# Expert routing by digits: where the running digit sum is formed and compared, and which engine makes some of the low weight parts

## The chip, the cores and the metric

The program runs on one core of a Trainium2 chip. The time is device microseconds of one execution. Five engines work at once, each through its own instructions in order: TensorE (PE in the profile, with PEld for its weight loads), VectorE (DVE), ScalarE (ACT), GpSimd (POOL) and SyncE (SP). TensorE writes its results to PSUM, which VectorE and ScalarE read.

## The reference

A bucketed attention makes 3072 tokens of 512 features, and a mixture of 8 experts works on them. Each expert takes at most 384 tokens: pairs of token and expert are visited from the highest logit down, and a token goes to the first expert that still has room.

```
x = attention(q, k, v, proj)                 # 3072 x 512, softmax within equal hash buckets
logits = x @ w_gate                          # 3072 x 8
for idx in argsort(-logits.flatten()):       # highest first
    tok, e = idx // 8, idx % 8
    if assigned[tok] >= 0 or counts[e] >= 384: continue
    assigned[tok] = e; counts[e] += 1
for e in range(8):
    h = maximum(x[assigned == e] @ w1[e], 0) # 384 x 1024
    out[assigned == e] = h @ w2[e]           # 384 x 512
```

## The kernel before

The first 403 us of the profiled execution are the attention and the logits. The diff adds only six small constants to that part. The rest is the mixture.

**Experts on TensorE.** `run` writes TensorE's program by hand: 68 slots per expert. In slots 0 to 31 `layer1` issues three matmuls of 128x384 each (four slots make one of eight pieces f of the hidden layer), in slots 32 to 67 `layer2` issues two of 128x512. Every product is made of half-precision high and low parts: for weights, `wsplit` lets ScalarE make the high part wh (L731) and scale the raw weights wf in place (L732), a quarter of a matrix at a time; the low part wl = wf - wh is made in halves of 512 columns by GpSimd (L743) or by VectorE (L747). The halves stand in the list `pend`: `hand` gives some of them to GpSimd behind a tiny copy ("tick") that waits for the latest comparison, and `fill` gives one to VectorE. The hidden piece f gets its high part hh from ScalarE (L783) and, four slots later (`lag`), its low part hl from VectorE (L784). The inputs xl (L757) are made likewise.

**Routing, one expert ahead.** While expert k's matmuls run, the generator `phase(k+1)` finds which tokens the next expert takes. It searches a threshold key in six digits (layers l = 0 to 5). Each digit is one loop round VectorE and TensorE: a comparison of the running value d with a table (`compare`, L497), a counting on TensorE (`count` for l = 0, `count4`, L515, for l = 1 to 5), three small subtractions (L517, L518), a test and a maximum (L593, L594) that give `hit`, and a matmul that sums `hit` over partitions (L597). From that sum n VectorE makes the new running value and compares again:

```
T.matmul(n,s.us[l][...],hit[...],start=True,stop=True)
V.scalar_tensor_tensor(d2,d,n,E[:,l+1],op0=ALU.subtract,op1=ALU.add)   # L603
s.compare(CMP[l+1],l+1,d2)
```

After the sixth counting (l = 5) come the last test (`satl`, L610), a matmul pair (L613, L614), a run of small VectorE steps to `cum` (L616 to L637), a matmul pair (L640, L641), the list of members (L649 to L662) and its collecting (L651), and the state for the next expert (L694, L667 to L673, then `best`).

**What sets the order.** The tables E1, EV, EO and ES say in which slot each of a phase's 14 to 18 pieces is issued; H1, H2 and HS how many halves GpSimd is handed after each; W1 and W2 in which slots ScalarE splits the quarters of the two matrices; XS and XD where the inputs are transposed. Each engine executes its share strictly in that order.

Of the kernel before, what the change touches and what calls it, by code (L numbers as in the profile page):

```python
# [378 lines left out]
SH=[25,20,15,10,5,0]  # L379
LOW=[1,1,1,1,1,0]  # L380
NT=[128,32,32,32,32,32]
E1=[-12,-4,-3,2,6,8,10,13,16,19,22,25,28,31,34,37,42,49]
H1=[0,0,0,0,0,2,0,2,0,2,0,3,0,3,0,0,0,0]
H2=[0,0,0,3,0,3,0,3,0,4,0,0,0,0]
EV=[0,0,-5,-8,-12]
ES=[-17,-14,-11,-8,-2,1,5,8,12,15,19,22,28,36]
EO=[0,3,6,9,13,16,20,23,27,30,34,37,43,51]
WL=[4,46]
W1=[[],[57,66,70,74],[53,65,69,73],[50,57,62,67],[46,52,58,63],[44,52,58,63]]
HS=[0,0,0,2,0,3,0,3,0,3,0,0,0,0]  # L390
# [8 lines left out]
class Moe:  # L399
    def __init__(s, tc, nc, ctx, N):  # L400
        s.tc,s.nc,s.N=tc,nc,N
        s.NC=NC=N//128; s.CAP=N//8
        s.cp=ctx.enter_context(tc.tile_pool(name="mcp",bufs=1)); s.zp=ctx.enter_context(tc.tile_pool(name="mzp",bufs=2))
        s.IDX={}; s.XG={}; s.W={}; s.WIX={}; s.late=[]; s.pend=[]; s.lag=[]; s.gate=None

    def consts(s):

# [135 lines left out]
    def phase(s,ph):  # L543
# [5 lines left out]
        def ps(): return s.ps0() if first and s.ps0 else s.ps()  # L549
# [3 lines left out]
        if not last:  # L553
# [13 lines left out]
            for l,w in enumerate(WID):  # L567
                tot+=w; u=2.0**-tot; cmp=CMP[l]
                yield
                pc=ps()  # L570
                if l==0 or first:
                    for c0,c1_ in blocks if first else ((0,NC),):
                        if l: s.compare(cmp,l,d,c0,c1_)
                        s.count(pc,P,cmp,l,c0,c1_)
                    if first:
                        if l==0: wp=s.wps(); s.warm(KW[7],wp)
                        s.warm(KW[0],wp)
                    for a,b in ((l+1,l+2),) if first else ((1,6),):
                        if a<6:
                            for q in range(a,b): s.digit(P,q,slice(0,NC))  # L580
                            if first: V.tensor_tensor(E[:,a:b],D[:,a:b],s.sc[:,a:b],op=ALU.mult)
                            else:
                                for q in range(a,b): nc.scalar.activation(E[:,q],D[:,q],AF.Copy,scale=2.0**-sum(WID[:q+1]))
                                if ph>3: s.fill()
                else:
                    nt=s.count4(pc,P,cmp)

                if l==5: break
                sat=t([128,8],BF,"sat"); hit=t([128,1],BF,"hit") if l==0 or first else s.hits[l%2]; J=NT[l]
                if l==0 or first:  # L590
                    V.tensor_scalar(sat[0:J],pc[0:J,0:8],0.0,0.0,op0=ALU.is_ge,op1=ALU.max,accum_out=hit[0:J])
                else:
                    V.tensor_tensor(sat[0:32],pc[96:128,24:32],nt,op=ALU.is_ge)  # L593
                    V.reduce_max(hit[0:32],sat[0:32],axis=AX.X)  # L594
                if not first: yield
                pn=ps(); n=pn[:,0:1]
                T.matmul(n,s.us[l][0:J if first else 128],hit[0:J if first else 128],start=True,stop=True)  # L597
                if first: s.warm(KW[1],wp)
                elif l==0 and ph>1:
                    s.fill()  # L600
                    if ph<4: s.fill()
                d2=t([128,NC],BF,"d2",bufs=6); s.gate=d2[0:1,0:1]
                V.scalar_tensor_tensor(d2,d,n,E[:,l+1],op0=ALU.subtract,op1=ALU.add)  # L603
                if not first:
                    s.compare(CMP[l+1],l+1,d2); s.gate=CMP[l+1][0:1,NC//2-1,0,0:1]
                d=d2

            sat=s.satl; s.gate=sat[0:1,0:1]; nn=t([128,1],F32,"nn"); nf=t([128,1],F32,"nf")
# [197 lines left out]
    def start(s):  # L806

        s.ps0=None; V=s.nc.vector
        s.wload(0,0,4,(0,1))
        next(s.ph0)  # L810
        s.gather(0)
        s.wload(0,0,4,(2,3))
        s.wsplit(0,0,0,V)
        next(s.ph0)
        s.ch=[s.phase(p) for p in range(8)]
        s.wsplit(0,0,1,V)
        s.wload(0,1,2)
        s.xsplit0()
        s.wsplit(0,0,2,by=14)
        s.wsplit(0,0,3,by=22)  # L820

    def run(s):
        V=s.nc.vector; ch=s.ch; at={}; NS=68
# [3 lines left out]
            if p<7: next(ch[p+1])  # L827
        def step(p,n):
            next(ch[p],None); s.hand(n)
        for p in range(1,8):  # L830
            b=NS*(p-1)
            c=[EV[p]+e for e in EO] if 1<p<5 else ES
            ev=[b+e for e in (E1 if p==1 else c)]
            hs=H1 if p==1 else H2 if p<4 else HS
            dec=ev[-3] if p<7 else b+24
            if p==7: ev=[b+28,b+40]; hs=[0,0]
# [4 lines left out]
                add(b+W1[min(p,5)][q],s.wsplit,p,0,q,None,b+NS+BY[0]+BY[1]*q if p<6 else 0)  # L841
                add(b+XS[q]+(XD[p] if p<4 else 0),s.xsplit,p,q)
        for k in range(8):
            for q in range(4): add(NS*k+W2[q],s.wsplit,k,1,q,None,NS*k+BY[2] if k<6 else 0)
            for q in range(3): add(NS*k+44+12*q+SC,s.scatter)
        for n in range(-NS,NS*8):
            s.now=n
            for f,a in at.get(n,()): f(*a)
            while s.lag and s.lag[0][0]<=n: s.lag.pop(0)[1]()
            while s.pend and s.pend[0][0]<=n: s.nc.gpsimd.tensor_tensor(*s.pend.pop(0)[1],op=ALU.subtract)  # L850
            if n<0: continue
            k,h=divmod(n,NS)
            if h<32: s.layer1(k,h//4,h%4)
            else: s.layer2(k,(h-32)//12,(h-32)%12)
# [53 lines left out]
```

## Time and profile before

| | |
|---|---|
| median of three runs | 749.07 us (747.76 to 753.79) |
| the profiled execution | 750.32 us, of which the trace spans 748.5 |
| TensorE matmul busy | 679.1 us, 91% of the span |
| VectorE, ScalarE, GpSimd busy | 541.0, 463.6, 511.7 us |
| mean granted TensorE clock | 0.969 |
| experts (from 433 us to the end of the span) | 315 us |

The engines work in parallel, so the busy times add up to more than the span. A matmul of 128x384 lasts 0.33 us from start to end, but the next one starts 0.16 us after it.

### The profile page before, as it was taken

To read this page: it belongs to the slowest core of one execution; us is meant where nothing else is said; L and a number is where in the kernel's file an instruction comes from. 1 tells how busy PE (TensorE), PEld (TensorE's weight loads), DVE (VectorE), ACT (ScalarE), POOL (GpSimd) and SP (SyncE) were. 2 spreads that over 40 slices of the span, in tenths; PEclk is the share of its full clock that TensorE was granted. 3 is DMA by queue.
4 is the path that set the end of the run, shared out by engine and by line. 5 is a ranking of instruction groups with operands and counts; after the bars stand their busy time and mean duration, and the time that the engine had idled before them with its cause. 6 is when DMAs were issued, how large, how long until landed. Compare 5 with 4: busy or idle time off the path is not lost. (4 is left out here: it accounts for less than half of the span.)

```text
span 748.5 us, 19027 instructions
## 1 busy us (share of the span) xinstructions
PE 679.1 (91%) x7789; PEld 437.9 (59%) x7789; DVE 541.0 (72%) x1162; ACT 463.6 (62%) x852; POOL 511.7 (68%) x452
## 2 busy tenths in 40 slices
PE   8898999999999999899997589999798999999995
PEld 2566666767667676677775454545445455555552
DVE  5879978887887899978875658586668878744120
ACT  7677676777767677566662171837456575666560
POOL 8686959798888878877663436575728392857671
PEclk9999999999999999999998589999999999999998
DMA  7638655427445264430000342525170717172611
GB/s 190 179 95 223 158 155 124 126 76 175 127 119 133 75 173 129 88 78 23 23 24 23 107 161 90 207 76 220 42 268 30 265 46 267 43 250 72 253 46 42
DMA packets 39951, 93.57 MB, mean 125 GB/s; under 512 B 4548, under 2 KB 30520, under 8 KB 37816
## 3 DMA queue, kind: packets, MB, share of 16 engines
q1 hardware_dynamic: 33048, 46.21, 23.7%
q0 software_dynamic: 6816, 46.15, 17.5%
q8 instruction: 61, 1.00, 0.6%
q14 instruction: 26, 0.21, 0.1%
HBM read 59.53 MB, written 12.58 MB: 96 GB/s over the span
## 5 line engine op out<-in xcount | busy, mean ns | idle before, releaser
L256 POOL TENSOR_TENSOR lo<-pt 128x768 f16<-128x768 f32 x143 | 234.5, 1652 | 57.0 <-ACT pt L253 48.6
L253 ACT ACTIVATE pt<-pst 128x384 f32<-128x384 f32 x384 | 182.9, 491 | 91.6 <-PE pst L252 78.0
L229 DVE TENSOR_REDUCE m<-pss 128x1 f16<-128x770 f32 x192 | 182.1, 956 | 35.8 <-PE pss L227 34.6
L251 PE MATMUL pst<-qa,ka 128*128 128x384 f16 x384 | 125.6, 327 | 3.3 <-DVE XT L295 1.8
L252 PE MATMUL pst<-qb,kb 128*128 128x384 f16 x384 | 125.3, 326 | 0.0
L268 PE MATMUL psv<-vh,lo 128*128 128x65 f16 x1152 | 121.4, 194 | 1.9 <-POOL lo L256 1.9
L267 PE MATMUL psv<-vl,pt 128*128 128x64 f16 x1152 | 121.7, 193 | 0.0
L266 PE MATMUL psv<-vh,pt 128*128 128x65 f16 x1152 | 121.6, 195 | 0.0
L266 PEld LDWEIGHTS <-pt 128*128 128x128 bf16 x1152 | 107.0, 98 | 12.7 <-issue 3.3
L267 PEld LDWEIGHTS <-pt 128*128 128x128 bf16 x1152 | 106.0, 99 | 9.4 <-issue 0.2
L268 PEld LDWEIGHTS <-lo 128*128 128x128 f16 x1152 | 106.1, 98 | 2.2 <-POOL lo L256 2.2
L227 PE MATMUL pss<-ka,qa 128*128 128x385 f16 x384 | 94.7, 329 | 12.3 <-DVE m L229 12.2
L731 ACT ACTIVATE wh<-wf 128x1024 f16<-128x1024 f32 x64 | 67.2, 1050 | 41.9 <-PE psa L699 21.1
L743 POOL TENSOR_TENSOR wl<-wf,wh 128x512 f16<-128x512 f32 x71 | 79.9, 1146 | 0.0
L781 PEld LDWEIGHTS <-wh 128*128 128x128 f16 x512 | 48.4, 99 | 39.0 <-issue 9.9
L732 ACT ACTIVATE wf<-wf 128x1024 f32<-128x1024 f32 x62 | 65.6, 1057 | 2.0
L784 DVE SCALAR_TENSOR_TENSOR hl<-px,hh 128x384 f16<-128x384 f32 x64 | 34.4, 552 | 43.0 <-ACT hh L783 42.6
L256 DVE TENSOR_TENSOR lo<-pt 128x768 f16<-128x768 f32 x49 | 63.5, 1297 | 1.5 <-ACT pt L253 1.0
L227 PEld LDWEIGHTS <-qa 128*128 128x128 f16 x384 | 37.3, 97 | 43.0 <-issue 20.2
L793 PEld LDWEIGHTS <-hh 128*128 128x128 f16 x384 | 36.4, 98 | 39.8 <-issue 1.8
L796 ACT ACTIVATE o<-po 128x512 f32<-128x512 f32 x24 | 14.2, 592 | 70.1 <-PE po L793 69.9
L781 PE MATMUL px<-xh,wh 128*128 128x384 f16 x256 | 54.3, 330 | 2.4 <-ACT wf L732 0.7
(253 smaller groups left out, 1327.0 us busy)
## 6 DMA issues: line engine op xcount, KB each, us to landing
vp<-in_vv_dram SPq DMA_DIRECT2D x8, 768.0 KB
x_dram<-X SPq DMA_DIRECT2D x16, 384.0 KB
qp<-in_qT_dram SPq DMA_DIRECT2D x7, 768.0 KB
kp<-in_kT_dram SPq DMA_DIRECT2D x7, 768.0 KB
qa<-qh SPq DMA_DIRECT2D x14, 192.0 KB
ka<-kh SPq DMA_DIRECT2D x14, 192.0 KB
qb<-qh SPq DMA_DIRECT2D x14, 192.0 KB
kb<-kh SPq DMA_DIRECT2D x14, 192.0 KB
```

Source lines behind the costliest of these rows:

```text
L227: T.matmul(ps[:,hf,0:HK],QA[u][:,j,qc*128:qc*128+128],KA[u][:,j,hf*HK:hf*HK+HK],start=True,stop=True)
L229: V.tensor_reduce(M6[h][:,qc:qc+1],ps[:,:,0:HK],axis=AX.XY,op=ALU.max,negate=True)
L251: T.matmul(ps[:,0:384],KA[u][:,j,kr],QA[u][:,j,r],start=True,stop=False)
L252: T.matmul(ps[:,0:384],KB[u][:,j,kr],QB[u][:,j,r],start=False,stop=True)
L253: A.activation(PT[h,kc][0][:,r],ps[:,0:384],AF.Exp,scale=0.125)
L256: eng.tensor_tensor(l,p,p.bitcast(BF)[:,1::2],op=ALU.subtract)
L266: T.matmul(av[:,c,:],ph[:,r],VH[u][:,j,kc,:],start=(kc==0 and c==0),stop=False,skip_group_check=True)
L267: T.matmul(av[:,c,0:64],ph[:,r],VL[u][:,j,kc,:],start=False,stop=False,skip_group_check=True)
L268: T.matmul(av[:,c,:],l[:,r],VH[u][:,j,kc,:],start=False,stop=False,skip_group_check=True)
L731: s.nc.scalar.mul(h[:,r],f[:,r],WSC)
L743: for _ in range(n): s.nc.gpsimd.tensor_tensor(*s.pend.pop(0)[1],op=ALU.subtract)
L781: T.matmul(p[:,0:384],a[:,o:o+128],b[:,d],start=n==0,stop=n==11)
```

## The change

In phases 1 to 7 the running value is no longer made by VectorE. TensorE adds up in one PSUM tile g: the old value d through an identity matrix `identb`, the next digit E[:,l+1] through the same, and minus the sum of `hit` through `nus`, spread over the 24 columns. VectorE compares g in PSUM with the table, then copies it to d2. The first two matmuls (`carry`) stand right behind the counting of a layer, for l = 0 behind its test. The digit E[:,1] is made by VectorE and no longer by ScalarE.

A second list `pendV` holds the low parts of eight quarters (`OWN`: the first quarter of layer 1 for experts 2 to 5, the fourth quarter of layer 2 for the same). VectorE makes them from the raw weights in one instruction, so ScalarE doesn't scale these quarters. `fill` takes from `pendV` first, and one half is taken behind the sixth counting, ahead of `satl`.

The tables move: the last two pieces of phases 1 to 3 stand one slot later, the first two of phases 5 to 7 too; layer 2's quarters of experts 0 to 2 are split later, and the fourth quarter of layer 1 for expert 0 moves from the start to slot 7; GpSimd is handed other numbers. In each slot what is due in `lag` now comes ahead of the pieces. Six small constants are made on GpSimd during the attention.

```diff
-E1=[-12,-4,-3,2,6,8,10,13,16,19,22,25,28,31,34,37,42,49]
+E1=[-12,-4,-3,2,6,8,10,13,16,19,22,25,28,31,34,37,43,50]
-H2=[0,0,0,3,0,3,0,3,0,4,0,0,0,0]
-EV=[0,0,-5,-8,-12]
-ES=[-17,-14,-11,-8,-2,1,5,8,12,15,19,22,28,36]
-EO=[0,3,6,9,13,16,20,23,27,30,34,37,43,51]
+H2=[0,0,0,3,1,3,1,3,1,3,0,0,0,0]
+ES=[-16,-13,-11,-8,-2,1,5,8,12,15,19,22,28,36]
...
-HS=[0,0,0,2,0,3,0,3,0,3,0,0,0,0]
+HS=[0,0,0,3,0,3,0,3,0,3,0,0,0,0]
-W2=[2,7,12,17]
+W2={0:[12,16,20,24],3:[2,7,12,17],1:[10,14,18,22],2:[6,11,16,21]}
+OWN=[(p,0,0) for p in range(2,6)]+[(k,1,3) for k in range(2,6)]
...
-                                for q in range(a,b): nc.scalar.activation(E[:,q],D[:,q],AF.Copy,scale=2.0**-sum(WID[:q+1]))
+                                V.tensor_tensor(E[:,a],D[:,a],s.sc[:,a],op=ALU.mult)
+                                for q in range(a+1,b): nc.scalar.activation(E[:,q],D[:,q],AF.Copy,scale=2.0**-sum(WID[:q+1]))
...
-                if l==5: break
+                def carry():
+                    g=ps()[:,0:NC]
+                    T.matmul(g,s.identb,d,start=True,stop=False)
+                    T.matmul(g,s.identb,E[:,l+1],start=False,stop=False)
+                    return g
+                if not first and 0<l<5: g=carry()
+                if l==5:
+                    if s.pendV: s.own()
+                    break
...
-                pn=ps(); n=pn[:,0:1]
-                T.matmul(n,s.us[l][0:J if first else 128],hit[0:J if first else 128],start=True,stop=True)
-                if first: s.warm(KW[1],wp)
-                elif l==0 and ph>1:
+                if first:
+                    pn=ps(); n=pn[:,0:1]
+                    T.matmul(n,s.us[l][0:J],hit[0:J],start=True,stop=True); s.warm(KW[1],wp)
+                else:
+                    if l==0: g=carry()
+                    T.matmul(g,s.nus[l],hit.to_broadcast([128,NC]),start=False,stop=True)
+                if l==0 and ph>1:
                     s.fill()
                     if ph<4: s.fill()
-                d2=t([128,NC],BF,"d2",bufs=6); s.gate=d2[0:1,0:1]
-                V.scalar_tensor_tensor(d2,d,n,E[:,l+1],op0=ALU.subtract,op1=ALU.add)
-                if not first:
-                    s.compare(CMP[l+1],l+1,d2); s.gate=CMP[l+1][0:1,NC//2-1,0,0:1]
+                d2=t([128,NC],BF,"d2",bufs=6)
+                if first: V.scalar_tensor_tensor(d2,d,n,E[:,l+1],op0=ALU.subtract,op1=ALU.add)
+                else:
+                    s.compare(CMP[l+1],l+1,g); V.tensor_copy(d2,g); s.gate=CMP[l+1][0:1,NC//2-1,0,0:1]
...
-        if eng is None: s.nc.scalar.mul(f[:,r],f[:,r],WSC)
+        own=by and (ph,which,q) in OWN
+        if eng is None and not own: s.nc.scalar.mul(f[:,r],f[:,r],WSC)
...
-            else: s.pend.append((by,a))
+            else: (s.pendV if own else s.pend).append((by,a))
...
-        if s.pend: s.nc.vector.tensor_tensor(*s.pend.pop(0)[1],op=ALU.subtract)
+        if s.pendV: s.own()
+        elif s.pend: s.nc.vector.tensor_tensor(*s.pend.pop(0)[1],op=ALU.subtract)
+    def own(s):
+        l,f,h=s.pendV.pop(0)[1]; s.nc.vector.scalar_tensor_tensor(l,f,WSC,h,op0=ALU.mult,op1=ALU.subtract)
...
             s.now=n
+            while s.lag and s.lag[0][0]<=n: s.lag.pop(0)[1]()
             for f,a in at.get(n,()): f(*a)
-            while s.lag and s.lag[0][0]<=n: s.lag.pop(0)[1]()
```

Three places show the order. In these rows zcmp is a comparison's result, zd the running value, psa a PSUM tile of the routing, znt the rest of the capacity after counting.

The first is VectorE at the last two layers of the phase that runs in expert 4. Before:

```order
L594 TENSOR_REDUCE hit_89<-zsat 32x1
L603 SCALAR_TENSOR_TENSOR zd_11052<-zd_11001,psa,zE 128x24
L497 TENSOR_TENSOR zcmp_384<-zd_11052,tb_100 128x768
L784 SCALAR_TENSOR_TENSOR hl<-px,hh 128x384
L517 TENSOR_TENSOR znt<-rem,psa 32x8
L518 TENSOR_TENSOR znt<-znt,psa 32x8 x2
L610 TENSOR_TENSOR satl<-psa,znt 32x8
L784 SCALAR_TENSOR_TENSOR hl<-px,hh 128x384
L616 TENSOR_REDUCE znn<-psa 128x1
```

And with the change (line numbers are those of the changed kernel; L503 is the comparison, L808 the hidden low part, L771 a low weight part):

```order
L609 TENSOR_REDUCE hit_89<-zsat 32x1
L808 SCALAR_TENSOR_TENSOR hl<-px,hh 128x384
L503 TENSOR_TENSOR zcmp_390<-psa,tb_101 128x768
L623 CAST zd_11123<-psa 128x24
L808 SCALAR_TENSOR_TENSOR hl<-px,hh 128x384
L523 TENSOR_TENSOR znt<-rem,psa 32x8
L524 TENSOR_TENSOR znt<-znt,psa 32x8 x2
L771 SCALAR_TENSOR_TENSOR wl_11023<-wf_10826,wh_11022 128x512
L628 TENSOR_TENSOR satl<-psa,znt 32x8
L634 TENSOR_REDUCE znn<-psa 128x1
```

The sum (L603) is gone ahead of the comparison, a cast stands behind it, and a weight half (L771) stands ahead of satl.

The second is ScalarE at the start of expert 2. The first wh named is layer 2's in the piece of before; L731 with L732 splits one quarter. Before:

```order
L731 ACTIVATE wh_9917<-wf_9752 128x1024
L732 ACTIVATE wf_9752<-wf_9752 128x1024
L783 ACTIVATE hh<-px 128x384
L731 ACTIVATE wh_9768<-wf_9642 128x1024
L732 ACTIVATE wf_9642<-wf_9642 128x1024
L731 ACTIVATE wh_9917<-wf_9752 128x1024
L732 ACTIVATE wf_9752<-wf_9752 128x1024
L783 ACTIVATE hh<-px 128x384 x2
L731 ACTIVATE wh_9917<-wf_9752 128x1024
L732 ACTIVATE wf_9752<-wf_9752 128x1024
L783 ACTIVATE hh<-px 128x384
```

And now, where wh_9806 belongs to layer 1 and wh_9995 to layer 2 (L749 with L751 splits a quarter, L807 makes hh):

```order
L749 ACTIVATE wh_9806<-wf_9681 128x1024
L751 ACTIVATE wf_9681<-wf_9681 128x1024
L807 ACTIVATE hh<-px 128x384
L749 ACTIVATE wh_9806<-wf_9681 128x1024
L751 ACTIVATE wf_9681<-wf_9681 128x1024
L749 ACTIVATE wh_9995<-wf_9792 128x1024
L751 ACTIVATE wf_9792<-wf_9792 128x1024
L807 ACTIVATE hh<-px 128x384
L749 ACTIVATE wh_9995<-wf_9792 128x1024
L751 ACTIVATE wf_9792<-wf_9792 128x1024
L807 ACTIVATE hh<-px 128x384 x2
```

Each quarter of layer 2 stands one hh later: the first has gone from ahead of the first hh to ahead of the second, the second from there to ahead of the third.

The third is VectorE at the end of the same expert's phase, from cum to the next indices. Before:

```order
L637 SCALAR_TENSOR_TENSOR zcum<-one_69,zSTb 128x48
L784 SCALAR_TENSOR_TENSOR hl<-px,hh 128x384
L747 TENSOR_TENSOR wl_9918<-wf_9752,wh_9917 128x512
L652 TENSOR_REDUCE zpm<-psa 128x24
L653 SCALAR_TENSOR_TENSOR zacc<-psa,zSTb 128x24
L655 TENSOR_SCALAR zmi<-zpm 128x24
L656 TENSOR_TENSOR zGt<-zpm,th 128x96
L657 TENSOR_SCALAR zmd<-zmi 128x24
L649 TENSOR_TENSOR ohp<-zmd,iot 128x3072
L675 TENSOR_TENSOR zRr<-zGt,gp 128x144 x2
L660 TENSOR_TENSOR zA_10125<-zwg,wt 128x192
L662 TENSOR_REDUCE zcc<-zA_10125 128x8
```

And now:

```order
L655 SCALAR_TENSOR_TENSOR zcum<-one_69,zSTb 128x48
L808 SCALAR_TENSOR_TENSOR hl<-px,hh 128x384 x2
L771 SCALAR_TENSOR_TENSOR wl_9996<-wf_9792,wh_9995 128x512
L670 TENSOR_REDUCE zpm<-psa 128x24
L671 SCALAR_TENSOR_TENSOR zacc<-psa,zSTb 128x24
L673 TENSOR_SCALAR zmi<-zpm 128x24
L674 TENSOR_TENSOR zGt<-zpm,th 128x96
L675 TENSOR_SCALAR zmd<-zmi 128x24
L667 TENSOR_TENSOR ohp<-zmd,iot 128x3072
L693 TENSOR_TENSOR zRr<-zGt,gp 128x144 x2
L678 TENSOR_TENSOR zA_10177<-zwg,wt 128x192
```

Both last hidden low parts (L808 x2) now stand ahead of the list of members; before, the last one (L784) stood behind it.

## Rows read from the trace of the kernel before

**Rows 1.** Waits of TensorE from 433 us: sum, times, longest (us).

```profile
PE psa L515 <- DVE zcmp L497: 6.2, 7, 2.2
PE po L793 <- DVE hl L784: 4.5, 3, 2.9
PE psa L597 <- DVE hit L594: 4.2, 3, 2.7
PE psa L640 <- DVE zwidx L706: 1.4, 3, 0.6
```

**Rows 2.** Timeline of TensorE, experts 0 to 2: start, us, instruction, idle before.

```profile
442.49 0.33 PE L515 MATMUL psa<-zOH,zcmp 128*128 128x32 bf16 x6 [2.19 <-DVE zcmp L497]
457.23 0.32 PE L515 MATMUL psa<-zOH,zcmp 128*128 128x32 bf16 x6 [0.62 <-DVE zcmp L497]
483.76 0.16 PE L597 MATMUL psa<-hit,us 128*128 128x1 bf16 x1 [0.80 <-DVE hit L594]
488.20 0.17 PE L597 MATMUL psa<-hit,us 128*128 128x1 bf16 x1 [0.70 <-DVE hit L594]
498.94 0.20 PE L640 MATMUL psa<-zSTb,ntri 128*128 128x48 bf16 x1 [0.59 <-DVE zwidx L706]
527.11 0.16 PE L597 MATMUL psa<-hit,us 128*128 128x1 bf16 x1 [2.69 <-DVE hit L594]
544.19 0.39 PE L793 MATMUL po<-wh,hl 128*128 128x512 f16 x1 [2.86 <-DVE hl L784]
```

**Rows 3.** The same timeline, experts 3 to 5; 648.30 repeats 611.60.

```profile
574.17 0.32 PE L515 MATMUL psa<-zOH,zcmp 128*128 128x32 bf16 x6 [0.92 <-DVE zcmp L497]
579.45 0.20 PE L640 MATMUL psa<-zSTb,ntri 128*128 128x48 bf16 x1 [0.52 <-DVE zwidx L706]
591.30 0.76 PE L508 MATMUL psa<-zOH,zcmp 128*128 128x8 bf16 x24 [0.98 <-DVE zcmp L497]
611.60 0.32 PE L515 MATMUL psa<-zOH,zcmp 128*128 128x32 bf16 x6 [0.86 <-DVE zcmp L497]
628.00 0.76 PE L508 MATMUL psa<-zOH,zcmp 128*128 128x8 bf16 x24 [0.39 <-DVE zcmp L497]
```

**Rows 4.** VectorE by line from 433 us: ns min/median/max, first and last start.

```profile
L603 DVE SCALAR_TENSOR_TENSOR zd<-zd,psa,zE x24: 236/249/2098, 445.8 to 645.5; 128x24 bf16<-128x24 bf16 x24
L497 DVE TENSOR_TENSOR zcmp<-zd,tb x30: 557/558/1382, 441.9 to 647.7; 128x768 bf16<-128x768 bf16 x30
L784 DVE SCALAR_TENSOR_TENSOR hl<-px,hh x64: 530/552/559, 441.1 to 725.0; 128x384 f16<-128x384 f32 x64
L747 DVE TENSOR_TENSOR wl<-wf,wh x21: 678/684/693, 473.6 to 659.0; 128x512 f16<-128x512 f32 x21
```

**Rows 5.** Timeline of VectorE, experts 0, 2 and 4.

```profile
441.13 0.56 DVE L784 SCALAR_TENSOR_TENSOR hl<-px,hh 128x384 f16<-128x384 f32 x1 [2.60 <-ACT hh L783]
525.68 0.56 DVE L784 SCALAR_TENSOR_TENSOR hl<-px,hh 128x384 f16<-128x384 f32 x1 [3.10 <-ACT hh L783]
608.84 2.04 DVE L603 SCALAR_TENSOR_TENSOR zd<-zd,psa,zE 128x24 bf16<-128x24 bf16 x1 [0.59 <-PE psa L597]
611.95 0.15 DVE L517 TENSOR_TENSOR znt<-rem,psa 32x8 f32<-32x8 f32 x1
613.74 0.30 DVE L619 SCALAR_TENSOR_TENSOR zwg<-zd,znn,zmxu 128x24 f32<-128x24 bf16 x1
```

**Rows 6.** Timeline of ScalarE at the start of expert 2.

```profile
520.73 0.47 ACT L783 ACTIVATE hh<-px 128x384 f16<-128x384 f32 x1
525.18 0.85 ACT L783 ACTIVATE hh<-px 128x384 f16<-128x384 f32 x2
```

**Rows 7.** Timeline of GpSimd in expert 4: runs of low weight parts.

```profile
607.46 3.38 POOL L743 TENSOR_TENSOR wl<-wf,wh 128x512 f16<-128x512 f32 x3
611.74 3.37 POOL L743 TENSOR_TENSOR wl<-wf,wh 128x512 f16<-128x512 f32 x3
```

**Rows 8.** Layer 1's matmuls by stretch: length, PE (count), PEld (count), clock, DMA, GB/s.

```profile
442.50:446.00 3.50, 3.35 (x11) 1.52 (x12) 0.52 0.00 0
446.00:449.50 3.50, 3.50 (x22) 1.80 (x20) 0.99 0.00 0
527.50:531.00 3.50, 3.50 (x14) 1.46 (x13) 0.57 0.02 5
```

More of the change, by code (lines that the diff above doesn't have):

```diff
@@ L381 @@
 NT=[128,32,32,32,32,32]
-E1=[-12,-4,-3,2,6,8,10,13,16,19,22,25,28,31,34,37,42,49]
+E1=[-12,-4,-3,2,6,8,10,13,16,19,22,25,28,31,34,37,43,50]
 H1=[0,0,0,0,0,2,0,2,0,2,0,3,0,3,0,0,0,0]
-H2=[0,0,0,3,0,3,0,3,0,4,0,0,0,0]
-EV=[0,0,-5,-8,-12]
-ES=[-17,-14,-11,-8,-2,1,5,8,12,15,19,22,28,36]
-EO=[0,3,6,9,13,16,20,23,27,30,34,37,43,51]
+H2=[0,0,0,3,1,3,1,3,1,3,0,0,0,0]
+ES=[-16,-13,-11,-8,-2,1,5,8,12,15,19,22,28,36]
+EP={1:E1,
[3 rows of a table added]
 WL=[4,46]
 W1=[[],[57,66,70,74],[53,65,69,73],[50,57,62,67],[46,52,58,63],[44,52,58,63]]
-HS=[0,0,0,2,0,3,0,3,0,3,0,0,0,0]
+HS=[0,0,0,3,0,3,0,3,0,3,0,0,0,0]
 BY=[-1,8,40]
-W2=[2,7,12,17]
+W2={0:[12,16,20,24],3:[2,7,12,17],1:[10,14,18,22],2:[6,11,16,21]}
+OWN=[(p,0,0) for p in range(2,6)]+[(k,1,3) for k in range(2,6)]
 XS=[56,56,57,57]
@@ L403, in __init__ @@
         s.cp=ctx.enter_context(tc.tile_pool(name="mcp",bufs=1)); s.zp=ctx.enter_context(tc.tile_pool(name="mzp",bufs=2))
-        s.IDX={}; s.XG={}; s.W={}; s.WIX={}; s.late=[]; s.pend=[]; s.lag=[]; s.gate=None
+        s.IDX={}; s.XG={}; s.W={}; s.WIX={}; s.late=[]; s.pend=[]; s.pendV=[]; s.lag=[]; s.gate=None
     def consts(s):
@@ L442, in consts @@
         s.hits=[fill([128,1],0.0,f"hit{i}",BF) for i in range(2)]; s.satl=fill([128,8],0.0,"satl",BF)
+        s.identb=cp.tile([128,128],BF,name="identb")
         s.gp=cp.tile([128,2,2,NC],BF,name="gp")
@@ L458, in consts @@
         s.rem=fill([128,8],float(s.CAP),"rem"); s.nrem=fill([128,8],-s.CAP/128.0,"nrem",F16)
+        todo.append(lambda: G_.tensor_scalar(s.identb,s.jp,0.0,None,op0=ALU.is_equal))
+        s.nus=[col(-2.0**-sum(WID[:l+1]),f"nus{l}") for l in range(5)]
         return todo
@@ L819, in start @@
         s.wsplit(0,0,2,by=14)
-        s.wsplit(0,0,3,by=22)
     def run(s):
@@ L829, in step @@
             next(ch[p],None); s.hand(n)
+        add(7,s.wsplit,0,0,3,None,22)
         for p in range(1,8):
             b=NS*(p-1)
-            c=[EV[p]+e for e in EO] if 1<p<5 else ES
-            ev=[b+e for e in (E1 if p==1 else c)]
+            ev=[b+e for e in EP.get(p,ES)]
             hs=H1 if p==1 else H2 if p<4 else HS
@@ L843, in run @@
         for k in range(8):
-            for q in range(4): add(NS*k+W2[q],s.wsplit,k,1,q,None,NS*k+BY[2] if k<6 else 0)
+            for q in range(4): add(NS*k+W2.get(k,W2[3])[q],s.wsplit,k,1,q,None,NS*k+BY[2] if k<6 else 0)
             for q in range(3): add(NS*k+44+12*q+SC,s.scatter)
@@ L847, in run @@
             s.now=n
+            while s.lag and s.lag[0][0]<=n: s.lag.pop(0)[1]()
             for f,a in at.get(n,()): f(*a)
-            while s.lag and s.lag[0][0]<=n: s.lag.pop(0)[1]()
             while s.pend and s.pend[0][0]<=n: s.nc.gpsimd.tensor_tensor(*s.pend.pop(0)[1],op=ALU.subtract)
+            while s.pendV and s.pendV[0][0]<=n: s.own()
             if n<0: continue
```

3 rows, old and new, of the table EP are left out of this document.

## Prediction

> **What bounds the kernel now.** I read the table of waits of the experts' part first. TensorE's sums there [rows 1] are small beside 315 us: TensorE works through its program, and only what makes it wait, slows its clock or adds matmuls can move the end. Then the timeline of TensorE, to see where each wait lies, and what VectorE, ScalarE and GpSimd did just before it. A matmul of 128x384 lasts 0.33 us and the next begins 0.16 us after it, so I count a wait as its bracket plus 0.16.
>
> The waits are of three kinds. In experts 0 to 2 [rows 2] the cause is mostly the order on VectorE and ScalarE: at 442.49 a counting came 2.35 us late and at 527.11 a sum of hits 2.85, each time behind a hidden low part (L784) that had itself waited 2.60 and 3.10 us for ScalarE's hh [rows 5]. At 544.19 layer 2 waited 3.02 us for the last hidden low part, which stood behind the list of members. In experts 3 to 5 [rows 3] the cause is GpSimd: the digit sum L603 lasts 0.249 us at the median and up to 2.098, the comparison L497 0.558 and up to 1.382, whereas L784 is never held over 0.559 [rows 4]. L603 and L497 read two operands from SBUF, L784 one from SBUF and one from PSUM. The third kind follows from the first: behind the waits of 442.49 and 527.11 the granted clock was 0.52 and 0.57, that is 1.2 instead of 2.4 GHz, and 11 and 14 matmuls of layer 1 went through in 3.5 us where 22 did at 0.99 [rows 8]. At 0.16 us each that cost (22-11) x 0.16 = 1.8 and 1.3 us; I use 1.5 and 1.3.
>
> **The change part by part.** The sum stands against the profiled execution, 750.3 us; the median lies 1.25 lower.
>
> Expert 0. The fourth quarter of layer 1 is split in slot 7 instead of ahead of the start, and layer 2's first from slot 12. A pair of splits takes ScalarE about 2.0 us: from the end of hh at 521.20 to the start of the next at 525.18 it does two [rows 6]. With one pair less ahead of it hh is on time for the wait at 442.49: 2.35 falls to some 0.25, -2.1, and the clock's drop behind it goes, -1.5. At 457.23 a comparison held by GpSimd cost 0.78. With one operand in PSUM I expect it not to be held, like L784: -0.8.
>
> The matmul L640 waited three times, 1.4 us in all [rows 1]. Two of these lie in phases whose last two pieces move by one slot, 0.49 us: 0.23+0.16 goes, and of 498.94's 0.59+0.16 all but 0.26 [rows 2]; -0.9. The third, 579.45 [rows 3], lies in phase 4, whose slots stay, and I leave it.
>
> Expert 1. The sums of hits at 483.76 and 488.20 came 0.96 and 0.86 late [rows 2], behind low parts whose hh stood behind splits of layer 2. These go from slots 2 and 7 to 10 and 14: -1.8.
>
> Expert 2. By the order each quarter of layer 2 stands one hh later on ScalarE, so the second hh comes one pair, 2.0 us, earlier: the wait of 2.85 falls to 0.85, -2.0, and a wait of that size had no drop behind it elsewhere, so its slow stretch goes, -1.3. For 544.19 the order shows both last hidden low parts ahead of the list of members. One weight half of 0.68 (L747, [rows 4]) still stands among these steps, so I leave 0.5 us: -2.5. I take its slow stretch, in layer 2, at 1.0, below both that rows 8 show: -1.0. The half behind the sixth counting costs 0.3 here, since GpSimd has little to do in this phase. Together -6.5.
>
> Experts 3 to 5. The waits of rows 3 other than 579.45, with 648.30 like 611.60, come to 1.08 + 1.14 + 1.02 + 0.55 + 1.02 = 4.8 us, all behind L603 or a comparison held by GpSimd: -4.8. But the weight half behind the sixth counting reads two operands from SBUF, ahead of satl, and here GpSimd is handed three halves after the same piece. I walk through expert 4: without the hold of 608.84 the comparison ends near 609.8, GpSimd's next run (now 611.74 to 615.11, [rows 7]) begins at 610.0 and lasts to 613.4, with instruction ends at 611.15 and 612.25; the weight half is due at 611.5. TensorE reaches the test at 612.25. Where the half gets through at 612.25, it ends at 612.9 and, with satl, TensorE waits 0.9; where only at 613.4, 2.05. The trace has both: L603 at 608.84 started 0.25 us behind a weight part's end at 608.59, waited past the one at 609.71 and ended at 610.88, with the run's end at 610.84; L619 at 613.74 lay across the instruction end at 613.99 and took 0.30 [rows 5, 7]. I take the middle, 1.5, three times: +4.5 (bounds 3 x 0 and 3 x 2.05). Queued behind this half on VectorE are satl, the hidden low part after it and the chain to L640; they are late by the same time, not more. Net -0.3.
>
> By the Trainium skill (SBUF — State Buffer, Who interferes with whom) a VectorE instruction with two SBUF inputs and a GpSimd instruction that reads SBUF shut each other out, and the second to issue waits until the first finishes; one with a single SBUF input does not contend. That L784 is never held agrees; that L603 at 608.84 was held past an instruction's end does not, and by the rule as it stands the sum would be lower by 1.8.
>
> The comparison. No row shows one of 768 elements from PSUM. L784 has 384 from PSUM in 0.552 us and L517 32x8 in 0.15 [rows 4, 5]: (0.552-0.15)/384 = 1.05 ns per element, so 0.96 us for 768. Bounds: 0.558 if nothing changes, 1.76 if an element of PSUM takes twice as long. Against 0.249 + 0.558 = 0.81 before, a round gets longer by 0.15. The copy to d2 lies behind the comparison, beside the counting. Rounds stand three or four slots apart in turn, so one that just fits three has 0.49 us left in four, 0.25 on average; some seven of the 30 have none (the waits for comparisons, [rows 1]): 7 x 0.15 = +1.0 (bounds 0 and 30 x 0.15 = 4.5).
>
> TensorE's new matmuls. Two identity matmuls for each of 30 rounds; the sum of hits is there already, only wider. Six matmuls of 128x32 begin and end within 0.32 us at 611.60 [rows 3]: (0.32-0.16)/5 = 0.03 each, 60 x 0.03 = +1.6 with weight loads rounded in (bounds 0, if they fall into waits, and 60 x 0.08 = 4.8, half their duration of 0.16 as with the large ones).
>
> At nothing I take: the six constants, under a microsecond of GpSimd beside the attention; E[:,1] on VectorE instead of ScalarE, one instruction like L517 in each phase (0 to +1); eight quarters that ScalarE doesn't scale, since nothing waits for ScalarE then; the later splits, whose cover is that layer 2 begins in slot 32 and the last split stands in slot 24, and that the same buffers are loaded anew only from slot 46; the numbers handed to GpSimd. If the cover of the splits failed, layer 2 would wait for low parts, about one GpSimd half of 1.13 us [rows 7].
>
> Sum: -2.1 -1.5 -0.8 -0.9 -1.8 -6.5 -0.3 +1.0 +1.6 = -11.3. 750.3 - 11.3 = 739.0 profiled, about 738 for the median.
>
> **The rivals.** One: the wait for GpSimd is moved, not removed. The weight half is held to the end of the run of three in experts 3 to 5 (2.05 instead of 1.5, +1.6), waits of that size are followed by a slow clock (3 x 1.3 = 3.9), and the remaining wait of expert 2 keeps its own (1.3). That gives 738 + 6.8, about 744.5. For it speaks that L603 was held to a run's end; against it that waits of up to 1.14 us had no slow stretch behind them, and that GpSimd's runs may fall elsewhere. Near the same time, 743.5, lies the case that the change doesn't do what it says: the comparison still reads its table from SBUF, and if that is enough to be held, 4.8 + 0.8 us come back. L784 with its one SBUF operand speaks against it.
>
> Two, on the slower side: the comparison from PSUM lasts 1.76 us, since f32 from PSUM, spread over 32 columns, may not run as L784's plain tile does. It is in each of 30 rounds, in the path from count to count: 30 x (1.76-0.81-0.25) = 21 in place of 1.0, that is 758. It decides from a comparison of 12.3/30 + 0.81 + 0.25 = 1.47 us on: there the gain is eaten. Against it speak 64 low parts at 0.53 to 0.56 us.
>
> Three: the hold of the weight half always ends with GpSimd's running instruction: 3 x 0.9 instead of 3 x 1.5, 736. L619 speaks for it, L603 against it. This is the Trainium skill's rule of above.
>
> **How the numbers follow.** Forecast 738: 0.50. Rival three: 0.12. Rival one with its neighbour: 0.30. Rival two: 0.08. The range leaves out rival two and the far ends: down to 731.5, where the weight half isn't held at all (-4.5) and the new matmuls fall into waits (-1.6); up to 746.5, rival one with 2 us more of the comparison's or matmuls' bounds. One per cent, 7.5 us, is about what a measurement of this kernel can tell from no change; the bounds are 741.6 and 756.6. Faster by more: 0.62; within: 0.31, with a little of rival two; slower: 0.07.
>
> **What would show it.** In the profile after, the comparison should stand near 0.96 us, with hardly any over 1.1 in experts 3 to 5; waits of over 2 us at the starts of experts 0 and 2 and ahead of the last hidden piece of expert 2 should be gone, with their half-clock stretches; the weight half should last 0.68 us in expert 2 and 1.3 to 2.6 in experts 3 to 5, with TensorE waiting 0.9 to 2 us at the test behind satl. The prediction is wrong if comparisons last over 1.4 us, if many rounds get waits of a few tenths, if the slow stretches stay or new ones follow satl, or if layer 2 waits for low parts.

## The result, and the profile after

The changed kernel takes 754.4 us (median of 12 runs, 750.89 to 758.84) against 749.02 (12 runs): a ratio of 1.0069, with a 95% interval of 1.0044 to 1.0094. It is slower, by less than 1%; 738 was forecast. The profiled execution has a span of 753.1 us, granted clock 0.963.

From the first matmul of expert 0 to the last of expert 7 the two traces give 306.3 us before and 312.1 after. By expert, from one first matmul of layer 1 to the next:

| expert | 0 | 1 | 2 | 3 | 4 | 5 | 6 | 7 |
|---|---|---|---|---|---|---|---|---|
| before, us | 43.2 | 39.8 | 44.5 | 40.2 | 36.7 | 35.2 | 34.9 | 31.9 |
| after, us | 39.4 | 40.8 | 41.5 | 40.1 | 42.3 | 40.3 | 35.4 | 32.3 |

So the gain at the start is there (-3.8 and -3.0 in experts 0 and 2), and experts 4 and 5 lose 5.6 and 5.1. The table of TensorE's waits of the changed kernel (sum, times, longest), to be held against [rows 1]:

```profile
PE psa L632 <- DVE satl L628: 11.5, 3, 4.6
PE psa L658 <- DVE zwidx L724: 4.5, 2, 2.7
PE psa L616 <- DVE hit L609: 1.7, 1, 1.7
PE psa L521 <- DVE zcmp L503: 1.4, 3, 0.7
PE psa L514 <- DVE zcmp L503: 1.0, 2, 0.6
```

The counting L521 and L514 (L515 and L508 before) waited 8.5 us in eleven waits before, and 2.4 in five now; the sum of hits L616 went from 4.2 to 1.7. In their place stand 11.5 us at the test (L632), where TensorE had never waited, and 4.5 at the matmul behind cum (L658). VectorE's view by line (ns min/median/max) shows that the comparison from PSUM is as worked out, and that the weight half is not:

```profile
L503 DVE TENSOR_TENSOR zcmp<-psa,tb x30: 947/958/959, 438.2 to 644.3; 128x768 bf16<-128x768 f32 x30
L623 DVE CAST zd<-psa x30: 172/173/174, 439.1 to 645.1; 128x24 bf16<-128x24 f32 x30
L771 DVE SCALAR_TENSOR_TENSOR wl<-wf,wh x16: 681/686/5368, 507.6 to 655.2; 128x512 f16<-128x512 f32 x16
```

The 30 comparisons take 0.947 to 0.959 us: none is held, against [rows 4]. The copy takes 0.173. A weight half takes 0.686 and up to 5.37. The timeline of VectorE in expert 4 shows one of the longest, where [rows 5] shows the same stretch before:

```profile
604.18 0.34 DVE L524 TENSOR_TENSOR znt<-znt,psa 32x8 f32<-32x8 f32 x2
604.45 5.35 DVE L771 SCALAR_TENSOR_TENSOR wl<-wf,wh 128x512 f16<-128x512 f32 x1
609.83 0.17 DVE L628 TENSOR_TENSOR satl<-psa,znt 32x8 bf16<-32x8 f32 x1
```

And GpSimd beside it, to be held against [rows 7] (L761 is the tick, L762 a weight half):

```profile
602.28 0.18 POOL L761 CAST ztick<-zcmp 1x1 f32<-1x1 bf16 x1
602.42 3.38 POOL L762 TENSOR_TENSOR wl<-wf,wh 128x512 f16<-128x512 f32 x3
605.75 0.17 POOL L761 CAST ztick<-zcmp 1x1 f32<-1x1 bf16 x1
605.89 3.36 POOL L762 TENSOR_TENSOR wl<-wf,wh 128x512 f16<-128x512 f32 x3
609.41 1.27 POOL L826 DMA_INDIRECT out_dram<-o,zidx  x1 [0.16 <-issue]
```

GpSimd is in a run of three halves when the weight half starts at 604.45. That run ends at 605.80, but the next tick and run are already queued, and VectorE gets through only when that too is over, at 609.25, 4.8 us after it started; it ends 0.55 us later. The tick of 605.75 copies a value of the comparison that had ended at 602.94, so GpSimd was 2.8 us behind VectorE. Before, it was the other way: the tick of the run at 611.74 had waited for the comparison:

```profile
611.61 0.17 POOL L742 CAST ztick<-zcmp 1x1 f32<-1x1 bf16 x1 [0.77 <-DVE zcmp L497]
```

The ticks' line from 433 us on says how long GpSimd sat idle ahead of them, and for what (us, times). Before:

```profile
  DVE zcmp L497: 47.4, 16
```

After:

```profile
  DVE zcmp L503: 39.9, 9
```

Of 25 ticks 16 waited for a comparison before; of 31 only 9 do now. Not all of that is the sums' doing: with them and GpSimd's numbers of before 14 of 25 still wait (run sums_alone, below), with the new slots as well 12 (sums_tables). In expert 1 no weight half stands ahead of satl, in expert 3 it slips through in 0.69 us, and zwg (L637), the next step with two tensors in SBUF, is held. VectorE in both experts:

```profile
489.33 4.66 DVE L637 SCALAR_TENSOR_TENSOR zwg<-zd,znn,zmxu 128x24 f32<-128x24 bf16 x1
568.54 3.47 DVE L637 SCALAR_TENSOR_TENSOR zwg<-zd,znn,zmxu 128x24 f32<-128x24 bf16 x1
```

GpSimd in expert 1, whose queue is empty at 493.94:

```profile
489.35 1.14 POOL L762 TENSOR_TENSOR wl<-wf,wh 128x512 f16<-128x512 f32 x1
490.58 3.36 POOL L762 TENSOR_TENSOR wl<-wf,wh 128x512 f16<-128x512 f32 x3
```

The waits bring slow stretches with them. Matmuls of layer 1 in the 3.5 us behind the waits of experts 4 and 5 (the columns are those of [rows 8]):

```profile
610.05:613.55 3.50, 3.47 (x11) 1.64 (x12) 0.50 0.20 75
652.35:655.85 3.50, 3.46 (x12) 1.70 (x13) 0.55 0.23 82
```

Again 11 and 12 where 22 would go, as in [rows 8]. The windows of the changed kernel show five such drops, three in layer 2: behind waits of 2.85, 2.35, 1.95, 4.8 and 4.8 us; before there were three.

### The profile page after: what moved, and what is told of

The parts are those of the page before. It is cut to its first block, busy times and chain, and to the rows that moved or that the text cites. A ratio compares the mean times of both kernels' runs of the same rounds, so it can differ in the third digit from the quotient of the medians.

```text
span 753.1 us, 19154 instructions
## 1 busy us (share of the span) xinstructions
PE 683.3 (91%) x7849; PEld 441.3 (59%) x7849; DVE 550.6 (73%) x1165; ACT 454.9 (60%) x838; POOL 515.9 (69%) x467
## 5 line engine op out<-in xcount | busy, mean ns | idle before, releaser
L227 PE MATMUL pss<-ka,qa 128*128 128x385 f16 x384 | 95.0, 329 | 11.7 <-DVE m L229 11.5
L749 ACT ACTIVATE wh<-wf 128x1024 f16<-128x1024 f32 x64 | 67.0, 1050 | 39.2 <-DMA wf<-in_w_dram,zwidx 37.0
L762 POOL TENSOR_TENSOR wl<-wf,wh 128x512 f16<-128x512 f32 x74 | 83.5, 1147 | 0.2 <-ACT wf L751 0.2
L808 DVE SCALAR_TENSOR_TENSOR hl<-px,hh 128x384 f16<-128x384 f32 x64 | 34.6, 553 | 39.2 <-ACT hh L807 38.5
L820 ACT ACTIVATE o<-po 128x512 f32<-128x512 f32 x24 | 14.2, 594 | 73.7 <-PE po L817 73.5
L751 ACT ACTIVATE wf<-wf 128x1024 f32<-128x1024 f32 x54 | 57.1, 1057 | 1.7
```

The lines of the kernel that those rows point to most:

```text
L227: T.matmul(ps[:,hf,0:HK],QA[u][:,j,qc*128:qc*128+128],KA[u][:,j,hf*HK:hf*HK+HK],start=True,stop=True)
L762: for _ in range(n): s.nc.gpsimd.tensor_tensor(*s.pend.pop(0)[1],op=ALU.subtract)
```

## The experiments

Theory H, formed from these rows: the loss is in the steps behind the sixth counting, where VectorE instructions that read and write only SBUF wait until GpSimd's queue is empty. Rival S: the wider sums, the longer comparison and the added matmuls cost something in each of 30 rounds. All times are medians, the ratio is to the kernel before, timed on the same chip.

**own_off.** The weight half behind the sixth counting is left out there; the halves are made at the next places where one is filled in.

```diff
-                if l==5:
-                    if s.pendV: s.own()
-                    break
+                if l==5: break
```

> The changed kernel without the weight half behind the sixth counting; the half waits for the next place where one is filled in. Theory H (holds): the changed kernel loses in the steps behind the sixth counting, where VectorE instructions with two SBUF operands are held by GpSimd's runs, to the end of the run. Then TensorE's three waits at the test (2.2 + 4.6 + 4.6 us) go, with the half-clock stretches behind two of them, but zwg takes the half's place: it is held by the same runs, and the matmul behind cum waits some 2 us in experts 4 and 5. Near 746, down from 754.4. Rival S (sums): the comparison from PSUM, the copy and the added matmuls cost a little in each of 30 rounds; then only three halves of 0.68 us go, and it stays at 752 or more.

Measured: 746.66 us, ratio 0.9979 (0.9949 to 1.0009); 7.7 us less than the changed kernel's median, and the two intervals lie apart. As theory H says: the wait at the test is gone, and zwg is held in its place. TensorE's waits (L656 is the matmul behind cum; L815, layer 2 of expert 2, waits for a weight half that VectorE now makes too late, which takes back some of the gain):

```profile
PE psa L656 <- DVE zwidx L722: 7.5, 4, 2.7
PE po L815 <- DVE wl L769: 2.0, 1, 2.0
```

VectorE in expert 4:

```profile
605.13 3.52 DVE L635 SCALAR_TENSOR_TENSOR zwg<-zd,znn,zmxu 128x24 f32<-128x24 bf16 x1
```

**hand_off.** GpSimd's halves of the tenth piece go to the twelfth.

```diff
-H2=[0,0,0,3,1,3,1,3,1,3,0,0,0,0]
+H2=[0,0,0,3,1,3,1,3,1,0,0,3,0,0]
-HS=[0,0,0,3,0,3,0,3,0,3,0,0,0,0]
+HS=[0,0,0,3,0,3,0,3,0,0,0,3,0,0]
```

> The changed kernel with the weight half where it is, but GpSimd gets its halves two pieces later: not behind the fifth comparison, behind cum. Theory H: in expert 4 and 5 the half is held only to the end of the run of three handed out earlier, so TensorE waits about 1.4 at the test instead of 4.6, zwg in experts 1 and 3 passes at once, their waits of 2.7 and 1.8 at the matmul behind cum go, and the list of members is held instead, at the price of about a microsecond in each of five experts: 743. Rival S: the numbers handed out don't matter, 752 or more.

Measured: 752.55, ratio 1.0055 (1.0027 to 1.0084). Theory H missed by 9.6 us, in the size of what it moved; the time is the one that rival S gave, but its reason is out, since the waits did move. Waits at the test fell to 3.3 and those behind cum went, but these waits of TensorE came:

```profile
PE psa L669 <- DVE zRr L693: 5.1, 4, 1.8
PE psa L616 <- DVE zsat L606: 2.7, 3, 1.6
PE px L779 <- DMA xg<-x_dram,zidx: 1.9, 4, 0.9
```

And on VectorE, in expert 4, these two steps of the list (0.18 us each elsewhere):

```profile
611.90 0.90 DVE L673 TENSOR_SCALAR zmi<-zpm 128x24 int32<-128x24 int32 x1
612.88 1.13 DVE L675 TENSOR_SCALAR zmd<-zmi 128x24 bf16<-128x24 f32 x1
```

The list of members has several small steps in SBUF, and each was held by another of GpSimd's halves; the list, the gathering of inputs and the next phase's first hits came late.

**sums_alone** and **tables_alone** split the change. The first is the kernel before with `carry`, the sum through `nus` and the comparison from g; the second is the kernel before with

```diff
-W2=[2,7,12,17]
+W2={0:[12,16,20,24],3:[2,7,12,17],1:[10,14,18,22],2:[6,11,16,21]}
-        s.wsplit(0,0,3,by=22)
+        add(7,s.wsplit,0,0,3,None,22)
```

with the new E1, ES and EP, and with `lag` ahead of the pieces.

> The kernel before with the PSUM sums and comparisons alone: slots, splits, GpSimd's numbers and the order in a slot as before, no quarters for VectorE alone. Theory H: the waits for L603 and held comparisons in experts 3 to 5 go (4.8 + 0.8), but the run of GpSimd behind the fifth comparison now holds zwg, about 2 us at the matmul behind cum in experts 1 to 5, some with a slow clock: 749 to 754, so the sums alone gain nothing. Rival S: 30 rounds get longer, 756 or more. If the sums were a plain gain, 744.

> The kernel before with the slots, the later splits of layer 2, the fourth quarter of layer 1 in slot 7 and the low parts ahead of the pieces; sums in SBUF, GpSimd's numbers as before, no quarters for VectorE alone. Theory H (what the prediction had right): the opening wait of expert 0 with its slow clock, the two of expert 1 and most of expert 2's go, 8 to 12 us: 737 to 741. Rival S says nothing else here; a rival of its own is that these waits come back elsewhere, because the experts' later part is bound by GpSimd: then 745 or more.

Measured: sums_alone 750.11, ratio 1.0031 (1.0002 to 1.006); tables_alone 741.81, 0.9925 (0.9892 to 0.9959). sums_alone is within theory H's range, tables_alone 0.8 us above it: the moved splits and slots bring some 6 to 7 us by themselves (5.6 by the ratio, 6.9 by the medians), the sums nothing: the interval of sums_alone lies just above 1. In sums_alone zwg is held in six phases, 1.05 to 2.84 us. In tables_alone the largest wait is the counting's, behind sums held as in [rows 4]:

```profile
PE psa L519 <- DVE zcmp L501: 8.6, 11, 1.1
```

**sums_tables** puts the two together, without the quarters that VectorE makes alone and with GpSimd's numbers of before.

```diff
-OWN=[(p,0,0) for p in range(2,6)]+[(k,1,3) for k in range(2,6)]
+OWN=[]
```

> The changed kernel with no quarters for VectorE alone, none behind the sixth counting, and GpSimd's numbers of before; that is tables_alone (741.8) with the sums in PSUM. Theory H: the waits of 8.6 us for held sums and comparisons that tables_alone has go, 1.8 us of added matmuls come, and zwg is held to the end of GpSimd's run behind the fifth comparison in four or five experts, some 2 us each at the matmul behind cum: 742 to 746, so the sums in PSUM gain nothing on these tables either. Rival P (plain gain): the sums in PSUM save what the timeline shows, 735 to 738, and only the halves and GpSimd's numbers did harm. Rival S: 748 or more.

Measured: 743.63, ratio 0.9922 (0.9889 to 0.9956). Within theory H's range: the sums add no gain to the tables. The wait behind cum is 4.7 us in five places.

**chain_psum** and **best1** take the second SBUF operand out of zwg and what follows.

```diff
-            wg=t([128,NC],F32,"wg"); e0=t([128,NC],F32,"e0"); ...
+            wg=t([128,NC],F32,"wg") if first else s.C[:,NC:2*NC]; mq=mxu if first else s.C[:,0:NC]; e0=t([128,NC],F32,"e0"); ...
-            V.scalar_tensor_tensor(wg,d,nn,mxu,op0=ALU.is_gt,op1=ALU.mult)
+            V.scalar_tensor_tensor(wg,d,nn,mq,op0=ALU.is_gt,op1=ALU.mult)
-        s.psX=ctx.enter_context(tc.tile_pool(name="mpsX",bufs=4,space=PS))
+        s.psX=ctx.enter_context(tc.tile_pool(name="mpsX",bufs=3,space=PS))
```

> own_off (746.7) with one SBUF operand less in each of the steps from zwg to cum: mxu, wg, a row of ones and the offset of the weights' rows stand in a PSUM bank, taken from the four of the hidden pieces (three are left, and the transposes stand one slot further apart). The work on GpSimd is untouched. Theory H: zwg and the steps behind it are no longer held, though GpSimd runs beside them, so the waits of 7.5 us at the matmul behind cum go; the list of members may be held a little longer instead: 739 to 742. If what counts is only that GpSimd is busy, or the length of the chain, nothing changes: 746 to 748.

> sums_tables with the steps from zwg to cum in PSUM as in chain_psum. Theory H: the two together take away the held sums, the held comparisons and the held zwg; left are 1.8 us of matmuls and the steps of the list of members: 736 to 739, faster than tables_alone. If the hold goes on to the list of members at full length, as in hand_off, 742 or more.

Measured: chain_psum 746.19, ratio 0.9976 (0.9946 to 1.0006), no better than own_off; best1 744.19, 0.9952 (0.9923 to 0.998), no better than sums_tables. Theory H missed both times: 746 to 748 was given for no effect at all, 742 or more for a hold that goes on to the list of members. The waits behind cum did fall, from 7.5 to 2.2 in chain_psum, but not to nothing, and a row of VectorE in its expert 1 says why:

```profile
492.16 4.16 DVE L641 TENSOR_SCALAR zSTb<-asg,zcm 128x24 bf16<-128x24 f32 x1
```

And TensorE's waits in chain_psum, at the transposes and behind cum:

```profile
PE px L779 <- DVE xl L781: 2.3, 3, 0.8
PE psa L658 <- DVE zwidx L724: 2.2, 1, 2.2
```

zwg, the sum asg and ze were not held any more. But zSTb (L641), with one tensor and a column of scalars, all in SBUF, was, for 4.16 us. Two tensors in SBUF are thus not needed for a hold. And the bank taken from the hidden pieces, or the moved transposes, cost 2.3 us at L779, so that the two effects can't be told apart in the time.

**spread** and **sums_spread** shorten GpSimd's runs.

```diff
-HS=[0,0,0,3,0,3,0,3,0,3,0,0,0,0]
+HS=[0,0,1,2,1,2,1,2,1,2,0,0,0,0]
```

H2 becomes the same; spread starts from own_off, sums_spread from sums_tables.

> own_off (746.7) with GpSimd's twelve halves handed out as one and two in turn, behind each piece from the third to the tenth, instead of three behind every second one. Theory H: a hold lasts to the end of what GpSimd has in its queue, and with twelve halves in 15 us GpSimd has hardly a gap, so shorter runs help zwg only a little: 744 to 747. Rival B (a hold ends with a run as it was handed out): zwg is held by two halves at most, 743 or less.

> sums_tables (743.6) with GpSimd's halves handed out as one and two in turn, as in spread. Theory H, as spread (741.1) corrected it (a hold ends with GpSimd's queue, and a shorter queue holds zwg for less): the waits of 4.7 us at the matmul behind cum fall by half or more: 739 to 741. If the quarters made by VectorE alone are what made spread fast, 743 or more.

Measured: spread 741.11, ratio 0.9903 (0.9875 to 0.993); sums_spread 741.34, 0.9882 (0.9843 to 0.9921). Theory H as it stood expected less of spread; rival B had the time, but not the reason: in the rows below zwg is held across the tick of 602.28, which parts two runs. Both beat the kernel before and the changed one, by 8 and 13 us. spread differs from own_off in GpSimd's numbers alone and takes 5.6 us less, with the intervals apart. The waits behind cum fell from 7.5 to 2.5, since GpSimd's queue is empty earlier (14.6 us after the first matmul of expert 4, 15.4 in own_off). TensorE's wait behind cum in sums_spread:

```profile
PE psa L656 <- DVE zwidx L722: 2.5, 3, 0.9
```

VectorE in its expert 4:

```profile
601.96 2.76 DVE L635 SCALAR_TENSOR_TENSOR zwg<-zd,znn,zmxu 128x24 f32<-128x24 bf16 x1
```

And GpSimd beside it:

```profile
602.28 0.17 POOL L759 CAST ztick<-zcmp 1x1 f32<-1x1 bf16 x1
602.42 2.25 POOL L760 TENSOR_TENSOR wl<-wf,wh 128x512 f16<-128x512 f32 x2
```

**tables_spread** and **own_spread** are the counter-tests: spread numbers on sums in SBUF, and spread with the weight half put back.

> tables_alone (741.8) with the same numbers for GpSimd; sums in SBUF. Theory H: the holds of L603 get shorter (at most two halves instead of three) but more pieces meet one, since GpSimd now works behind every piece: 740 to 743. Against sums_spread it shows what the sums in PSUM are worth where GpSimd's queue is short: by theory H 0 to 2 us in their favour.

> spread (741.1) with the weight half behind the sixth counting put back, that is the changed kernel with GpSimd's numbers spread and nothing else. Theory H: the half is held to the end of the queue, now 1.5 to 2.8 us instead of 4.7, and zwg behind it is not: satl and the test are later by that, some 1 to 2 us in experts 2, 4 and 5, less what zwg no longer waits: 742 to 745, 10 us faster than the changed kernel. If the half itself is at fault and not what it meets, 748 or more.

Measured: tables_spread 744.42, ratio 0.993 (0.9899 to 0.9961); own_spread 751.18, 1.0014 (0.9985 to 1.0043). Both are over their range, own_spread at the time given for the half itself being at fault. Spreading brings nothing with the sums in SBUF: the ratios of tables_alone and tables_spread are the same, and the wait for held sums is longer, 14.0 against 8.6. With the sums in PSUM it is 3.1 us less by the medians, but the intervals of tables_spread and sums_spread touch, so what the sums are worth there isn't settled. What the weight half alone costs is settled: 751.2 against 741.1, with the intervals well apart (8 us by the ratios). TensorE's largest wait in tables_spread:

```profile
PE psa L519 <- DVE zcmp L501: 14.0, 13, 2.3
```

In own_spread:

```profile
PE psa L632 <- DVE satl L628: 10.6, 4, 3.9
```

VectorE in expert 4 of own_spread:

```profile
604.29 4.61 DVE L771 SCALAR_TENSOR_TENSOR wl<-wf,wh 128x512 f16<-128x512 f32 x1
```

Why the half is so much dearer than zwg, which meets the same queue: in expert 4 GpSimd's queue is empty 14.6 us after the expert's first matmul in sums_spread (604.67 against 590.07) and in own_spread (608.35 against 593.75) alike, and 15.3 or 15.4 in the changed kernel and own_off. With the sums in PSUM, who is held, and for how long, doesn't change that end (with the sums in SBUF, in tables_spread, it is 15.5, and GpSimd's last tick waits 0.84 us for a comparison). So own_spread's half is held for 4.61 us and not for the 1.5 to 2.8 that theory H gave it: that estimate was wrong, not the hold. With the half ahead of satl, TensorE stands at the test, in slot 22, until then. Without it satl passes, and TensorE works on to slot 28, some 3 us further, before it needs cum.

## Why the prediction was wrong

**The step that failed** is the walk through expert 4 in the part on experts 3 to 5: "GpSimd's next run (now 611.74 to 615.11, [rows 7]) begins at 610.0 and lasts to 613.4", and with it the bounds "3 x 0 and 3 x 2.05". It moved GpSimd's run forward with the comparison, by 1.7 us. But GpSimd had idled only 0.77 ahead of that run: by [rows 7] the run before it, of 607.46, ends at 610.84, so that nothing could begin at 610.0. And "the numbers handed to GpSimd" stood at nothing, without a reason, though the change hands it one half more ahead of that, 1.13 us. A start at 612 and an end at 615.4 would have put the hold at 4 us. The runs show both shares: from the first matmul of expert 4 to the end of GpSimd's last half it is 14.2 us before, 13.5 with the sums in PSUM alone (sums_alone, 0.7 less and not 1.7), 14.3 in sums_tables, where the slots moved too, and 15.3 with the change's numbers.

Measured: waits of 4.6 in experts 4 and 5 and 2.2 in expert 2, 12.0 us with 0.16 each, where +4.5 and, for expert 2, +0.3 were in the sum. In expert 2 the half was to cost little "since GpSimd has little to do in this phase"; the change's numbers put single halves between the runs there, and it lasted 2.94 us. Rival one named the mechanism, but with the same bound, so it too ended 10 us short. The changed trace is 15.9 us longer than the sum has it (+4.6 against -11.3): 7.2 of them are waits at the test and 3.8 waits behind cum. The slow clock is likely most of the rest, but no run shows it by itself.

**A term that was missing:** the steps behind satl. With the sums held no longer, zwg arrives while GpSimd still has a run or more ahead of it: 4.66 us in expert 1 and 3.47 in expert 3. The trace before already had such a hold, in expert 3 (L619 is zwg there):

```profile
576.30 2.43 DVE L619 SCALAR_TENSOR_TENSOR zwg<-zd,znn,zmxu 128x24 f32<-128x24 bf16 x1
```

TensorE's wait behind cum rose from 1.4 to 4.5, where -0.9 stood. own_off shows the same term without the half: 7.5.

**The slow clock** was taken off for three stretches, and came back five times. The sentence "a wait of that size had no drop behind it elsewhere" spoke of a wait of 0.85; the one left there was 1.9 and had no drop either, but 1.95 us in expert 3 had one. That new slow stretches follow satl stood among the prediction's own signs of being wrong.

**What was right.** The comparison: 0.958 us, worked out as 0.96, so rival two is out. No comparison is held; that the change does what it says is shown. The waits for held sums [rows 3] fell as forecast, and with them the waits of the countings, 8.5 to 2.4. Expert 0: -3.8 against -2.1 - 1.5 - 0.8 - 0.4 and a share of the new matmuls. Expert 1 up to the sixth counting: layer 1 is 1.7 shorter, against -1.8. Expert 2: the wait of 544.19 is gone; that of 527.11 is still 1.9, not 0.85. tables_alone shows these parts by themselves: 6 to 7 us.

**What was right by luck.** Of the five waits of [rows 3] that the prediction puts down to GpSimd, two had another cause. At 591.30 and 628.00 the counting L508 waited for the first comparison of a phase, of 3072 elements, which was not held: it takes 1.75 us each time, and GpSimd did nothing but issue DMAs beside it. VectorE before 591.30:

```profile
589.49 1.75 DVE L497 TENSOR_TENSOR zcmp<-zE,tb 128x3072 bf16<-128x3072 bf16 x1
```

In sums_alone, with the sums in PSUM and the old slots, both waits are still there, 0.98 and 0.39 us; the first:

```profile
590.17 0.76 PE L514 MATMUL psa<-zOH,zcmp 128*128 128x8 bf16 x24 [0.98 <-DVE zcmp L503]
```

In tables_alone, with the new slots and sums in SBUF, one is down to 0.55 and the other gone. So these 1.7 of the -4.8 us came from the new slots for the most part, and not from the sums in PSUM, whose worth the prediction put too high.

**The new matmuls.** Three rows of the changed kernel, one behind the other on TensorE:

```profile
562.60 0.17 PE L597 MATMUL psa<-zd,identb 128*128 128x24 bf16 x1
562.63 0.17 PE L598 MATMUL psa<-zE,identb 128*128 128x24 bf16 x1
562.65 0.65 PE L805 MATMUL px<-xl,wh 128*128 128x384 f16 x3
```

0.03 us from start to start, as estimated: 60 x 0.03 = 1.8, where the prediction wrote +1.6. (Its lower end has a slip too: 738 - 4.5 - 1.6 is 731.9.) The longer round shows no cost beyond that, as few countings wait. Rival S can't explain the loss, since own_off, with all sums and matmuls in it, takes 7.7 us less.

**The rule.** By the Trainium skill (SBUF — State Buffer, Who interferes with whom) the second instruction waits until the first finishes. In the changed kernel the held weight half of expert 4 sat through the ends of four of GpSimd's instructions and a tick between them, and that of expert 5 likewise. In hand_off most were released at the next end. What decides between the two stays open. The same section of the Trainium skill excepts the 2-port perf modes from what it says of a single SBUF input, and names tensor_scalar among the operations that can enter them; the prediction left that out. Both zSTb (L641) and the zmi of hand_off (L673) are tensor_scalars, so their holds don't contradict it; in which mode they ran no run here shows.

**Open as well:** what the change's numbers for GpSimd cost against those of before. own_off and sums_tables differ in them and in the eight quarters for VectorE, by 3.0 us of their medians, and their intervals overlap. The quarters by themselves show no effect where GpSimd's halves are spread: spread and sums_spread differ in them alone and take 741.11 and 741.34.

## What to carry to other kernels

A held instruction is also a clock for the engine that holds it: when a hold is taken away, the next instruction that can be held meets more of the queue behind it, so ask where that queue ends, not how long one of its runs is. An engine can start earlier by no more than it idled: GpSimd had 0.77 us ahead of the run that the prediction moved by 1.7. And of work that must be done beside such a queue, put it behind the step that TensorE needs next: here a half of 0.7 us ahead of the test, in each of four experts, cost 7 to 10 us in all.

## What the runs showed of the hardware

Which VectorE instructions are held beside GpSimd's tensor instructions isn't told by the number of SBUF operands alone. Held: zwg, asg and the comparison (two tensors in SBUF), and also zSTb in chain_psum (one tensor and a column of scalars) and zmi (one tensor and constants; 0.90 us in hand_off, and 2.33 at 687.61 in the trace before, against 0.18). Not held, though they start and end inside one of GpSimd's instructions: hit from sat, a maximum along 8 columns in SBUF (17 of 17 in the trace before, at most 0.153 us), znf, one column from one column (6 of 6, at most 0.156), and everything with an operand in PSUM but L603, which has two more in SBUF (up to 2.098 us [rows 4]).

A held instruction can sit through the tick of 0.18 us between two of GpSimd's runs, so that one of 0.69 us lasted 5.35.
